# Folding the first head pair's decay terms into the 88-row contraction of its q k product

## The chip, the cores and the metric

The kernel runs on one core of one Trainium2 chip. A core has five engines that run side by side, each with its own instruction stream: TensorE (PE in the profile) for matrix products, VectorE (DVE), ScalarE (ACT), GpSimd (POOL) and SyncE (SP). POOL, SP and ACT also issue DMA transfers, which move data between the chip's memory and the on-chip buffers. The metric is the time of one execution on the device in microseconds (us), lower is better; a version's time is the median of its runs.

## The reference, cut to what matters

```python
scores = scale * np.matmul(q, k.transpose(0, 1, 3, 2))      # q, k, v: 8 batches, 8 heads, 576 tokens, 64 wide
log_f = np.log(np.clip(f, 0.0001, 1.0))                     # f: 8 x 8 x 576, a forget gate for each head and token
cum = np.cumsum(log_f, axis=-1)
decay = cum[:, :, :, None] - cum[:, :, None, :]
scores = np.where(causal, -1000000000.0, scores + decay)
attn = softmax(scores)                                      # (written out in the reference, with + 1e-09)
x = (attn @ v), heads side by side                          # 4608 tokens x 512
h = x @ w_in                                                # w_in: 512 x 2048
out = (h - np.tanh(h)) @ w_out                              # w_out: 2048 x 512, out: 4608 x 512 float32
```

What matters here is `decay`: to the score of query i and key j, cum at i is added and cum at j is taken away, for each head of each batch.

## The kernel before, in words

**Pairs and tiles.** The 64 heads (8 batches of 8) are worked in 32 pairs of heads. For a pair, q and k are transposed so that the 64 numbers of a head stand on 64 partitions (`trans`, L254 to L282: TensorE transposes at L264, then copies by VectorE or ScalarE at L275 and L277 into the tiles QT and KT). Scores are made key block by key block, transposed (keys on partitions), in seven tiles of a pair (TILES, L289), each of up to 512 columns in one PSUM bank (`scores`, L306): one product k q for each part of a tile (L326), in batch 0 a second small one that adds a mask to the diagonal blocks (L329, `late`), then exp by ScalarE (L335). `values` (L350) multiplies with v, VectorE normalises (L364 to L366), `turn` (L369) transposes the result into XR, and the MLP (`mlp1` L398 to L417, `mlp2_plain` and `mlp2` from L436) follows, spread between later pairs.

**The decay, from the second pair on.** QT and KT have three rows more than the 64 of the head: rows 64 to 66. KT has cum there in two fp16 parts (chi, the rounded value, and clo, the rest) and a row of ones; QT has two rows of -1 and a row cq with cum less a shift. One product over 67 rows so gives scale, decay and all. The constant rows come by SP's queue (L175 to L179), the others by `load_aug` (L168), for batch 0 on POOL's queue: from partition (batch, head) to row 64, 65 or 66 of every head.

**The decay, in the first pair.** These rows come too late for the first pair (`own`, L319). There the product runs over the 64 rows alone, and two matmuls for each part put the decay into PSUM first (`decay_part`, L294 to L298): one with the tile `dec` (chi and clo on 128 partitions) against a column `sel` that picks the head and changes the sign, one with a column of the identity against cq. The first tile's two are issued ahead (`decay(0)`, L529).

**The front.** f is loaded to 64 partitions (batch, head) by SP (L123), clipped by VectorE (L150), Ln by ScalarE (L157), summed up by a scan on VectorE (L159), rounded to chi (L162) and clo (L166); cq is made by ScalarE (L524). ScalarE needs a table load ahead of Ln and another ahead of exp (L525). `unread(n)` (L512) issues n matmuls of 128 columns whose result nobody reads, into which waits of TensorE fall.

**What sets the order.** Each engine works its instructions in the order in which the program emits them: `start()` (L521) emits the front and the first two tiles of pair 0, `bulk()` (L181) the rest of batch 0's loads, and then `att_items(p)` (L547) gives pair p's items: its seven tiles, the transposes of the next pair (`at_q` and `at_k` say behind which tile), loads (LOADS, L196) and the values of the pair before. POOL's queue in this order: q and k of heads 0 and 1 (L124, L125), of heads 2 and 3 (L132, L133), v of the last block and of heads 0 and 1 (L144 to L146), then `bulk`: q of heads 4 to 7, the three rows of `load_aug(0)` (chi L171, cq L172, clo L173), k of heads 4 to 7, four blocks of v; then batch 1's q and k, and w_in's first half (L189, placed at pair 1's tile 2). The first MLP matmul (L408) stands in pair 4's items behind tile 1.

Lines that say what words can't:

```python
    def load_aug(b):
        i, hs = b % 2, slice(b * H, (b + 1) * H)
        eng = nc.gpsimd if b == 0 else nc.sync
        eng.dma_start(out=KT[i][D:D + 1, :, 0:S], in_=chi[hs, :])
        eng.dma_start(out=QT[i][D + 2:D + 3, :, :], in_=cq[hs, :])
        eng.dma_start(out=KT[i][D + 1:D + 2, :, 0:S], in_=clo[hs, :])
```

Of the kernel before, what the change touches and what calls it, by code (L numbers as in the profile page):

```python
# [21 lines left out]
def kernel(  # L22
# [95 lines left out]
    def load_v_block(b, n, h0, h1):  # L118
# [3 lines left out]
    lf = TQ[0][0:NH, :, :].rearrange("p c s -> p (c s)").bitcast(FP32)[:, 0:S]  # L122
    nc.sync.dma_start(out=lf, in_=f.rearrange("b h s -> (b h) s"))  # L123
# [10 lines left out]
    ones16 = TK[0:NH, 0, :]  # L134
    sel = cst.tile([P, 2], FP16)
    dec = cst.tile([P, PITCH], FP16)
# [5 lines left out]
    nc.vector.memset(dec[:, S:PITCH], 0.0)  # L142
# [6 lines left out]

    nc.vector.tensor_scalar(out=lf, in0=lf, scalar1=0.0001, scalar2=1.0,  # L150
                            op0=ALU.max, op1=ALU.min)

    nc.vector.scalar_tensor_tensor(out=sel, in0=id16[:, 0:2], scalar=-1.0, in1=id16[:, NH:NH + 2],
                                   op0=ALU.mult, op1=ALU.subtract)
    nc.vector.memset(vn[0][D:P, NJ - 1, :, :], 0.0)
    nc.vector.memset(vn[0][:, :, :, D:VW], 1.0)
    nc.scalar.activation(out=lf, in_=lf, func=AF.Ln)  # L157
    cum = TQ[0][0:NH, :, :].rearrange("p c s -> p (c s)").bitcast(FP32)[:, S:2 * S]
    nc.vector.tensor_tensor_scan(out=cum, data0=ones16, data1=lf, initial=0.0,  # L159
                                 op0=ALU.mult, op1=ALU.add)  # L160
    chi = dec[0:NH, 0:S]
    nc.vector.tensor_scalar_mul(out=chi, in0=cum, scalar1=inv_qscale)  # L162
    cq = cst.tile([NH, S], FP16)
    expo = cst.tile([1, 1], FP32)
    clo = dec[NH:2 * NH, 0:S]
    nc.vector.scalar_tensor_tensor(out=clo, in0=cum, scalar=inv_qscale, in1=chi,  # L166
                                   op0=ALU.mult, op1=ALU.subtract)
    def load_aug(b):  # L168
        i, hs = b % 2, slice(b * H, (b + 1) * H)
        eng = nc.gpsimd if b == 0 else nc.sync  # L170
        eng.dma_start(out=KT[i][D:D + 1, :, 0:S], in_=chi[hs, :])  # L171
        eng.dma_start(out=QT[i][D + 2:D + 3, :, :], in_=cq[hs, :])  # L172
        eng.dma_start(out=KT[i][D + 1:D + 2, :, 0:S], in_=clo[hs, :])  # L173
# [120 lines left out]
    def decay_part(ps, a, j, i0, n, col):  # L294
        nc.tensor.matmul(out=ps[:, col:col + n], lhsT=dec[:, j * P:(j + 1) * P],
                         rhs=sel[:, a:a + 1].to_broadcast([P, n]), start=True, stop=False)
        nc.tensor.matmul(out=ps[:, col:col + n], lhsT=id16[0:NH, a:a + 1].to_broadcast([NH, P]),  # L297
                         rhs=cq[:, i0:i0 + n], start=False, stop=False)  # L298

    FIRST = []  # L300

    def decay(ti):
        FIRST.append(ps_sc.tile([P, 512], FP32, tag="sc", name="ps"))
        decay_part(FIRST[0], *TILES[ti][0])

    def scores(b, c, ti):  # L306
        if FIRST:
            ps = FIRST.pop()
        elif b == 0 and ti == LAST:
            ps = ps_tr.tile([P, UW], FP32, tag="tr", name="ps")  # L310
        else:
            ps = ps_sc.tile([P, 512], FP32, tag="sc", name="ps")
# [6 lines left out]
        own = b == 0 and c == 0  # L319
        rows = D if own else D + 3  # L320
        for a, j, i0, n, col in TILES[ti]:
            h = 2 * c + a
            if own and ti > 0:
                decay_part(ps, a, j, i0, n, col)
            cut = min(P, n) if b == 0 and i0 == j * P else 0
            nc.tensor.matmul(out=ps[:, col:col + n], lhsT=KT[b % 2][0:rows, h, j * P:(j + 1) * P],  # L326
                             rhs=QT[b % 2][0:rows, h, i0:i0 + n], start=not own, stop=cut == 0)
# [67 lines left out]
    def widen(n):  # L395
        turn_of[:] = [n, 0]
# [124 lines left out]
    def start():  # L521
        unread(33)
        q_rest = trans(*pairs[0], qn, QT, True, "AAAA", True)
        nc.scalar.activation(out=cq, in_=cum, func=AF.Copy, bias=-SHIFT * inv_qscale, scale=inv_qscale)  # L524
        nc.scalar.activation(out=expo, in_=lf[0:1, 0:1], func=AF.Exp)  # L525
        unread(6)
        k_rest = trans(*pairs[0], kn, KT, True, "VVVV", True)
        unread(22)
        decay(0)  # L529
        unread(8)  # L530
        scores(*pairs[0], 0)
        for fn in k_rest:
            fn()
        q_rest[0]()
        scores(*pairs[0], 1)
        q_rest[1]()
        for e in EL[0:2]:
            nc.vector.memset(e, 0.0)
        nc.vector.memset(KT[0][:, :, S:PITCH], 0.0)
# [7 lines left out]
    def att_items(p):  # L547
# [8 lines left out]
        for ti in range(len(TILES)):  # L556
# [5 lines left out]
            if early and p > 0 and ti in (0, 6):  # L562
                put(unread, 2)
# [4 lines left out]
            at_q, at_k = (1, 3) if p == 0 else (0, 1) if early else (0, 2) if p == NPAIR else (0, 3)  # L568
# [34 lines left out]
    FIVE = {PE, mybir.EngineType.Pool, mybir.EngineType.SP, mybir.EngineType.DVE, mybir.EngineType.Activation}  # L603
    with tc.manual_schedule(engines=FIVE):
        start()
    with tc.manual_schedule(engines=FIVE):
        bulk()
        for p in range(len(pairs) + 1):
            b, c = divmod(p, NPAIR)
            items = att_items(p)  # L610
            take = TAKE[p] if p < len(TAKE) else 8 - (p - len(TAKE)) % 2
            if p == 2 * NPAIR + 1:
                widen(1)
            mine = mlp[at:at + take]
            at += take
            first = 14 if p == NPAIR else 0
# [44 lines left out]
```

## Time and profile before

| | |
|---|---|
| median of 3 runs | 348.01 us (348.01 to 348.04) |
| the profiled execution | 347.95 us, of it 346.2 from the first to the last instruction (the span) |
| TensorE clock granted | 1.00 in every window |
| chain that ended last, by engine | PE 87%, DVE 6%, ACT 4% |
| same, by line, the largest | L408 32%, L466 28%, L326 12%, L357 8% |
| DMA | 38.80 MB, mean 112 GB/s |

The profile is that of one execution. For each engine it gives the busy time; the timeline gives instructions in order of time, each with its start, its length, its engine and line, the tile written and read, how many like it were merged, and in brackets how long the engine was idle ahead of it and what released it. The chain of waits is followed back from the last instruction and tells which work the end hung on. "PEld" is TensorE's load of the stationary operand, which may run beside a matmul. A line such as L408 is a line of the kernel as printed above.

### The profile page before, as it was taken

What the parts mean: (1) busy time and instruction counts of PE and PEld (TensorE: products, weight loads), DVE (VectorE), ACT (ScalarE), POOL (GpSimd) and SP (SyncE); (2) the same over time, 40 slices, a digit from 0 to 9 for tenths busy, and PEclk for the clock granted to TensorE, in tenths of its full rate; (3) what the DMA queues carried; (4) which work ended last, traced back from release to release, by engine and by line L of the source; (5) the groups of instructions that cost most, each with busy time, mean ns of one, the idle gap of its engine ahead of it and who ended that gap; (6) DMA issues with size and microseconds to landing.
All of it is one profiled execution on the core that took longest, in us unless ns stands there. A gap on an engine that the chain in (4) does not pass through costs nothing.

```text
span 346.2 us, 8606 instructions
## 1 busy us (share of the span) xinstructions
PE 335.2 (97%) x3253; PEld 230.6 (67%) x3253; DVE 261.7 (76%) x504; ACT 232.6 (67%) x437; POOL 161.3 (47%) x319
## 2 busy tenths in 40 slices
PE   8988998889999999999999999999999999999995
PEld 7476554555578656865688888755875587487485
DVE  6599787564988788678867886788677766876874
ACT  5687886777897787778767876788548842632640
POOL 8974652676558655765577465742322210000000
PEclk9999999999999999999999999999999999999999
DMA  8999999999999999799979997991131013003003
GB/s 108 147 182 201 193 201 154 107 114 177 132 130 105 177 137 122 94 176 137 117 78 200 130 128 78 186 143 27 49 97 31 17 50 110 0 14 109 0 11 113
DMA packets 144877, 38.80 MB, mean 112 GB/s; under 512 B 128148, under 2 KB 143236, under 8 KB 144836
## 3 DMA queue, kind: packets, MB, share of 16 engines
q0 software_dynamic: 92480, 18.39, 69.7%
q1 hardware_dynamic: 52356, 19.88, 30.5%
q8 instruction: 25, 0.41, 0.5%
q14 instruction: 16, 0.13, 0.1%
HBM read 36.85 MB, written 9.44 MB: 134 GB/s over the span
## 4 chain that ended last, share of the span: by engine, by line
PE 87%; DVE 6%; ACT 4%; issue 1%; DMA 1%; ACTq 0%
PE hps L408 32%; PE ops L466 28%; PE ps L326 12%; PE av L357 8%; PE ops L442 3%; DVE gq L417 2%; ACT e L335 2%; DVE QT L277 2%; PE t L264 1%; DVE KT L277 1%; PE ps L329 1%; DMA TQ<-in_f_dram 1%; PE ps L297 1%; ACT QT L275 1%; ACT th L413 1%
## 5 line engine op out<-in xcount | busy, mean ns | idle before, releaser
L408 PE MATMUL hps<-XR,win 128*128 128x512 f16 (+1 forms) x640 | 140.9, 357 | 0.9 <-ACT XR L378 0.7
L413 ACT ACTIVATE th<-hps 128x512 f32<-128x512 f32 x144 | 86.9, 603 | 55.4 <-PE hps L408 54.6
L335 ACT ACTIVATE e<-ps 128x512 f16<-128x512 f32 x192 | 110.5, 598 | 14.1 <-PE ps L326 6.0
L417 DVE TENSOR_TENSOR gq<-hps,th 128x512 f16<-128x512 f32 x144 | 98.4, 688 | 26.0 <-ACT th L413 24.6
L345 POOL TENSOR_SCALAR_AFFINE_SELECT e<-e 128x128 f16<-128x128 f16 x168 | 60.4, 361 | 78.0 <-ACT e L335 76.1
L408 PEld LDWEIGHTS <-win 128*128 128x128 f16 x640 | 57.7, 97 | 48.4 <-issue 0.5
L326 PE MATMUL ps<-QT,KT 67*128 67x64 f16 (+5 forms) x384 | 77.9, 276 | 3.1 <-ACT e L335 1.7
L466 PEld LDWEIGHTS <-gq 128*128 128x128 f16 x640 | 60.4, 97 | 11.1
L466 PE MATMUL ops<-wout,gq 128*128 128x256 f16 x512 | 63.2, 272 | 0.0
L326 PEld LDWEIGHTS <-KT 67*128 67x128 f16 (+1 forms) x384 | 36.7, 98 | 25.5 <-DVE KT L277 1.6
L357 PEld LDWEIGHTS <-e 128*128 128x128 f16 x896 | 32.2, 97 | 3.9
L357 PE MATMUL av<-vn,e 128*128 128x65 f16 x896 | 33.6, 193 | 0.0
L119 POOL DMA_DIRECT2D vn<-in_v_dram x32 | 28.0, 878 | 8.7 <-DMA win<-in_moe_w_in_dram 4.1
L466 PE MATMUL ops<-W,sq 128*128 128x256 f16 x256 | 31.2, 272 | 0.0
L366 DVE TENSOR_TENSOR xn<-av,rs 128x640 f16<-128x640 f32 x32 | 26.4, 825 | 1.1
L466 PEld LDWEIGHTS <-sq 128*128 128x128 f16 x256 | 24.2, 98 | 3.4
L96 POOL DMA_DIRECT2D kn<-in_k_dram x25 | 21.2, 848 | 1.5 <-issue 1.3
L345 POOL TENSOR_SCALAR_AFFINE_SELECT el<-el 128x128 f16<-128x128 f16 x28 | 9.4, 334 | 26.9 <-ACT el L335 26.2
L96 POOL DMA_DIRECT2D qn<-in_q_dram x25 | 21.2, 848 | 1.3 <-issue 0.8
L364 DVE TENSOR_SCALAR rs<-av 128x10 f32<-128x10 f32 x32 | 5.2, 162 | 19.0 <-PE av L357 17.9
L277 DVE COPY QT<-t 64x576 f16<-64x576 f16 x18 | 14.5, 803 | 6.2 <-PE t L264 6.1
L277 DVE COPY KT<-t 64x576 f16<-64x576 f16 (+1 forms) x22 | 16.3, 739 | 3.8 <-PE t L264 3.6
(82 smaller groups left out, 307.5 us busy)
## 6 DMA issues: line engine op xcount, KB each, us to landing
out_dram<-ost SPq DMA_DIRECT2D x34, 256.0 KB
vn<-in_v_dram POOLq DMA_DIRECT2D x24, 128.0 KB, 5.6
qn<-in_q_dram POOLq DMA_DIRECT2D x20, 128.0 KB, 4.3
kn<-in_k_dram POOLq DMA_DIRECT2D x20, 128.0 KB, 4.6
win<-in_moe_w_in_dram POOLq DMA_DIRECT2D x2, 1024.0 KB, 14.8
wout<-in_moe_w_out_dram POOLq DMA_DIRECT2D x2, 1024.0 KB, 14.1
XR<-xn SPq DMA_TRANSPOSE x56
vn<-in_v_dram POOLq DMA_DIRECT2D x12, 64.0 KB, 5.2
```

What stands on the lines that cost most here:

```text
L96: nc.gpsimd.dma_start(out=dst[b % 2][0:pn, n, :].rearrange("p (h d) -> p h d", h=H), in_=src[b, :, n * P:n * P + pn, :].rearrange("h p d - ...
L119: nc.gpsimd.dma_start(out=vn[b % 2][:, n, h0:h1, 0:D], in_=v[b, h0:h1, n * P:(n + 1) * P, :].rearrange("h p d -> p h d"))
L277: nc.vector.tensor_copy(out=to, in_=of)
L326: nc.tensor.matmul(out=ps[:, col:col + n], lhsT=KT[b % 2][0:rows, h, j * P:(j + 1) * P], rhs=QT[b % 2][0:rows, h, i0:i0 + n], start=not ow ...
L335: nc.scalar.activation(out=e[:, lo:hi], in_=ps[:, lo:hi], func=AF.Exp, scale=qscale)
L345: nc.gpsimd.affine_select(out=view, in_=view, compare_op=ALU.is_ge, fill=0.0, base=0, pattern=pat, channel_multiplier=-1)
L357: nc.tensor.matmul(out=av[:, a, ib, :], lhsT=E.pop((b, c, a, j, ib)), rhs=vn[b % 2][:, j, 2 * c + a, 0:D + 1], start=(j == 0), stop=(j == ib))
L366: nc.vector.tensor_tensor(out=xn.rearrange("p i (a d) -> p a i d", a=2), in0=av[:, :, :, 0:D], in1=rs.to_broadcast([P, 2, NJ, D]), op=ALU. ...
L408: nc.tensor.matmul(out=hps[:, o:o + n], lhsT=win[:, ci, ft * P:(ft + 1) * P], rhs=XR[:, ci, t:t + n], start=(ci == 0), stop=(ci == NCH - 1))
L413: nc.scalar.activation(out=th, in_=hps, func=AF.Tanh, scale=-1.0)
L417: nc.vector.tensor_tensor(out=GQ[(u, i)][:, half, kt, :], in0=hps, in1=th, op=ALU.add)
L466: nc.tensor.matmul(out=ps[:, m, :], lhsT=LHS[lhs](u, kt // 4)[:, kt % 4, m * P:(m + 1) * P], rhs=rhs[:, kt, :], start=(fresh and (apart or ...
```

## The change: one contraction over 88 rows

For the first pair, the 64 rows of the head and 24 rows of decay terms stand in one tile, so that one product over 88 rows gives the whole score, and the two decay matmuls of each part go. The 24 rows are made where they are needed: f's eight rows of batch 0 are loaded a second time, three times over, to partitions 64 to 87, by ScalarE's queue; clip, Ln and scan run over 88 partitions instead of 64. Three groups of eight rows follow: on K's side -chi, ones, clo (by per-partition factors mul_k, add_k, mul_l), the same for both heads; on Q's side for head h a one in row h of the first group, cum less the shift in row h of the second, a -1 in row h of the third, and zeros elsewhere (by mul_0, add_0, mul_1, add_1). The factors are made from the identity tile by eleven small VectorE operations. The first pair's operands are KS and QS, which lie in the space of the weights W1 and W2 that are filled later. Also: `load_aug` issues clo ahead of cq; clo is made by VectorE after the first two copies of k; the exp table load stands right behind Ln; K's padding memset stands at the front; the transposes of k for pair 2 stand behind pair 1's tile 3 instead of tile 1; and the idle matmuls are 91 instead of 69 up to pair 1.

```diff
+    NX = NH + 3 * H
+    lf = TQ[0][0:NX, :, :].rearrange("p c s -> p (c s)").bitcast(FP32)[:, 0:S]
+    nc.sync.dma_start(out=lf[0:NH, :], in_=f.rearrange("b h s -> (b h) s"))
+    nc.scalar.dma_start(out=lf[NH:NX, :], in_=bass.AP(f.tensor, f.offset, [[0, 3], [S, H], [1, S]]))
...
+    nc.vector.memset(KT[0][:, :, S:PITCH], 0.0)
+    chi = cst.tile([NX, S], FP16)
+    clo = cst.tile([NH, S], FP16)
+    cq = cst.tile([NH, S], FP16)
+    KS = W1.rearrange("p k e -> p (k e)")[:, 0:2 * PITCH].rearrange("p (a n) -> p a n", a=2)
+    QS = W2.rearrange("p k e -> p (k e)")[:, 0:2 * S].rearrange("p (a n) -> p a n", a=2)
+    nc.vector.memset(KS[0:NX, :, S:PITCH], 0.0)
+    per = cst.tile([NX, 9], FP32)
+    isb, isc, mul_k, add_k, mul_l, mul_0, add_0, mul_1, add_1 = (per[:, i:i + 1] for i in range(9))
...
+    for to, i in ((isb, H), (isc, 2 * H)):
+        nc.vector.tensor_reduce(out=to, in_=id16[0:NX, NH + i:NH + i + H], op=ALU.add, axis=mybir.AxisListType.X)
+    nc.vector.tensor_scalar(out=mul_k, in0=isb, scalar1=-inv_qscale, scalar2=inv_qscale, op0=ALU.mult, op1=ALU.add)
+    nc.vector.tensor_scalar_mul(out=add_k, in0=isb, scalar1=-1.0)
+    nc.vector.tensor_scalar_mul(out=mul_l, in0=isc, scalar1=inv_qscale)
     nc.vector.tensor_scalar(out=lf, in0=lf, scalar1=0.0001, scalar2=1.0, op0=ALU.max, op1=ALU.min)
-    nc.vector.scalar_tensor_tensor(out=sel, in0=id16[:, 0:2], scalar=-1.0, in1=id16[:, NH:NH + 2], ...)
     nc.vector.memset(vn[0][:, :, :, D:VW], 1.0)
+    for h, (mul, add) in enumerate(((mul_0, add_0), (mul_1, add_1))):
+        nc.vector.tensor_scalar_mul(out=mul, in0=column(H + h), scalar1=inv_qscale)
+        nc.vector.scalar_tensor_tensor(out=add, in0=mul, scalar=-SHIFT, in1=column(h), op0=ALU.mult, op1=ALU.add)
+        nc.vector.tensor_tensor(out=add, in0=add, in1=column(2 * H + h), op=ALU.subtract)
     nc.scalar.activation(out=lf, in_=lf, func=AF.Ln)
+    nc.scalar.activation(out=expo, in_=lf[0:1, 0:1], func=AF.Exp)
     nc.vector.tensor_tensor_scan(out=cum, data0=ones16, data1=lf, ...)
-    nc.vector.tensor_scalar_mul(out=chi, in0=cum, scalar1=inv_qscale)
-    nc.vector.scalar_tensor_tensor(out=clo, in0=cum, scalar=inv_qscale, in1=chi, op0=ALU.mult, op1=ALU.subtract)
+    nc.vector.tensor_scalar(out=chi, in0=cum, scalar1=mul_k, scalar2=add_k, op0=ALU.mult, op1=ALU.add)
+    nc.vector.scalar_tensor_tensor(out=KS[NH:NX, 0, 0:S], in0=cum[NH:NX, :], scalar=mul_l[NH:NX, :], in1=chi[NH:NX, :],
+                                   op0=ALU.mult, op1=ALU.subtract)
     def load_aug(b):
         eng.dma_start(out=KT[i][D:D + 1, :, 0:S], in_=chi[hs, :])
+        eng.dma_start(out=KT[i][D + 1:D + 2, :, 0:S], in_=clo[hs, :])
         eng.dma_start(out=QT[i][D + 2:D + 3, :, :], in_=cq[hs, :])
-        eng.dma_start(out=KT[i][D + 1:D + 2, :, 0:S], in_=clo[hs, :])
...
     def scores(b, c, ti):
+        kt, qt, rows = (KS, QS, NX) if b == 0 and c == 0 else (KT[b % 2], QT[b % 2], D + 3)
         for a, j, i0, n, col in TILES[ti]:
-            if own and ti > 0:
-                decay_part(ps, a, j, i0, n, col)
+            nc.tensor.matmul(out=ps[:, col:col + n], lhsT=kt[0:rows, h, j * P:(j + 1) * P],
+                             rhs=qt[0:rows, h, i0:i0 + n], start=True, stop=cut == 0)
...
     def start():
+        def row_q(h, mul, add):
+            nc.scalar.activation(out=QS[NH:NX, h, :], in_=cum[NH:NX, :], func=AF.Identity, bias=add[NH:NX, :], scale=mul[NH:NX, :])
         unread(33)
-        q_rest = trans(*pairs[0], qn, QT, True, "AAAA", True)
-        nc.scalar.activation(out=cq, in_=cum, func=AF.Copy, ...)
-        nc.scalar.activation(out=expo, in_=lf[0:1, 0:1], func=AF.Exp)
+        row_q(0, mul_0, add_0)
+        q_rest = trans(*pairs[0], qn, (QS,), True, "AAAA", True)
+        row_q(1, mul_1, add_1)
+        nc.scalar.activation(out=cq, in_=cum[0:NH, :], func=AF.Copy, ...)
         unread(6)
-        k_rest = trans(*pairs[0], kn, KT, True, "VVVV", True)
-        unread(22)
-        decay(0)
-        unread(8)
+        k_rest = trans(*pairs[0], kn, (KS,), True, "VVVV", True)
+        unread(32)
         scores(*pairs[0], 0)
+        unread(4)
+        nc.vector.scalar_tensor_tensor(out=clo, in0=cum[0:NH, :], scalar=inv_qscale, in1=chi[0:NH, :], ...)
+        nc.vector.tensor_copy(out=KS[NH:NX, 1, 0:S], in_=KS[NH:NX, 0, 0:S])
         for fn in k_rest:
             fn()
         q_rest[0]()
         scores(*pairs[0], 1)
+        unread(4)
         q_rest[1]()
...
-            if early and p > 0 and ti in (0, 6):
-                put(unread, 2)
+            if early and ti in (0, 6) or p == 0 and ti == 5:
+                put(unread, 2 if p else 4)
-            at_q, at_k = (1, 3) if p == 0 else (0, 1) if early else ...
+            at_q, at_k = (1, 3) if p == 0 else (0, 3) if p == 1 else (0, 1) if early else ...
```

The whole program now stands under one hand-ordered schedule instead of two after the front (`manual_schedule`).

## The prediction

> **What bounds the kernel now.** I read the page first, then the chain of waits, then the timeline of the first 60 us by engine. Part 1 of the page says TensorE is nearly always busy:
>
> ```profile
> PE 335.2 (97%) x3253; PEld 230.6 (67%) x3253; DVE 261.7 (76%) x504; ACT 232.6 (67%) x437; POOL 161.3 (47%) x319
> ```
>
> That is an average. The change touches the first pair alone, so only the first 17 us and what they start matter. The timeline there (start, us, engine, line; in brackets the idle time before and its releaser):
>
> ```profile
> 0.81 1.28 ACT L157 ACT_TABLE_LOAD   x1 [0.81 <-PEq L645]
> ...
> 3.55 0.54 DVE L150 TENSOR_SCALAR TQ<-TQ 64x576 f32<-64x576 f32 x1 [0.71 <-DMA TQ<-in_f_dram]
> ...
> 4.11 0.68 ACT L157 ACTIVATE TQ<-TQ 64x576 f32<-64x576 f32 x1 [2.02 <-DVE TQ L150]
> ...
> 4.83 1.35 DVE L159 TENSOR_TENSOR_SCAN TQ<-TK,TQ 64x576 f32<-64x576 f16 x1 [0.66 <-ACT TQ L157]
> ...
> 6.96 0.75 DVE L166 SCALAR_TENSOR_TENSOR dec<-TQ,dec 64x576 f16<-64x576 f32 x1
> ...
> 7.82 1.96 DVE L277 COPY KT<-t 64x288 f16<-64x288 f16 x4
> ...
> 9.96 0.70 POOL L90 DMA_DIRECT2D kn<-in_k_dram  x1
> ...
> 13.32 0.39 PE L297 MATMUL ps<-cq,id 64*128 64x512 f16 x1
> ```
>
> Read down: up to 7.9 us a chain of f, clip, Ln, scan and two roundings runs. From then to 16.23, where pair 1 starts, TensorE itself is the chain, two decay matmuls like that of L297 ahead of each product. From there VectorE sets the pace: its copies of successive pairs start at 17.07, 21.56 and 26.05, that is 4.49 us per pair with 99% busy. The last fact is the one that I take to decide. POOL's timeline, its idle time, and the load's time to landing (last column):
>
> ```profile
> 16.67 0.83 POOL L189 DMA_DIRECT2D win<-in_moe_w_in_dram  x1
> ...
> 30.79 0.82 POOL L119 DMA_DIRECT2D vn<-in_v_dram  x1 [4.11 <-DMA win<-in_moe_w_in_dram]
> ```
> ```profile
> win<-in_moe_w_in_dram POOLq DMA_DIRECT2D x1, 1024.0 KB, 13.8
> ```
> ```profile
> 31.98 0.81 PE L408 MATMUL hps<-XR,win 128*128 128x512 f16 x3
> ```
>
> The first half of w_in lands at 16.67 + 13.8 = 30.47 and the first MLP matmul, which needs it, starts at 31.98 without idle time: 1.5 us of room, no more. Behind that matmul the chain goes through TensorE, ACT and VectorE to 56.6 us, then TensorE to the end, so the total moves with the start of that matmul.
>
> **TensorE's work in pair 0.** 24 decay matmuls go. In the chain from 0 to 18 us L295 has 9.1% and L297 14.4%: 1.64 + 2.59 = 4.2 us. 22 more idle matmuls come (91 for 69), at 1.39/22 = 0.063 us each 1.4 us; ten of them stand ahead of the first score in a wait that is there anyway (below), twelve between scores. The 88-row product takes no longer than the 64-row one: the 512-column form with 67 rows takes 0.38, the one with 64 rows 0.39. So TensorE alone would save some 3 us in pair 0. If nothing else bound, that would be the gain.
>
> **The front gets later.** In the instruction order of the changed kernel the Ln table load now waits for both landings of f; before it ran at 0.81, free. f landed at 3.52 (0.81 + 2.71 in the chain). The 24 repeated rows go out on ACT's queue; I let them land with the others, since SP's 64 rows issue at the same 0.81. Then the load takes 3.55 to 4.83 and Ln starts at 4.85 instead of 4.11. Eleven small VectorE operations on 88x1 are new. The nearest rows are 128x10: 0.17 and 0.22, 0.21 to 0.25 from start to start when one needs the other; the bottom is the 0.09 of a small memset. Five stand ahead of the clip, hidden by the table load; six stand between clip and scan, where Ln (to 5.53) hides most. The scan then starts between 5.56 and 6.1; I take 5.75. From there: scan 1.38, chi 0.73, the 24-row subtraction 0.75 (as the 64-row form), two head-0 copies of k 0.98, clo 0.75. The sum puts the end of **clo at 10.35** (bounds 10.15 to 10.7; it was 7.71) and the first score near 9.65 instead of 9.14. ACT does the second table load (1.28), two new 24x576 rows (0.66 as cq), two copies and cq by about 10; so its first exp slips from 9.72 to about 10.1.
>
> The Trainium skill ("ScalarE: Activation LUTs", What ACT_TABLE_LOAD costs) gives 1.28 us for a load and 1.38 us more for a drain at each switch. By that sentence Ln, and with it clo, would come 1.4 us later still; here the load at 7.47 is followed by an activation at 8.77, so this trace shows the 1.28 alone.
>
> **Pair 0 and pair 1.** VectorE follows clo with the copy of the 24 rows to head 1 (not in the trace: between 0.11 for a memset and 0.75 for an operation of that length; 0.4), the head-1 copies 0.98, memsets 0.24, and the copies for pair 1, 1.61 + 1.60. That ends at 15.2, where pair 1 may start: 1.0 us before 16.23. The memset of K's padding moved ahead of f, where VectorE waits (0.71 idle), and costs nothing. Pair 1 also needs cq's rows by POOL's DMA: issue near 10.9, landing 3.4 (fastest v load) to 5.1 (cq now) later, 14.3 to 16.0. So pair 1 gains 0.2 to 1.05, and I take 1.0 because few loads are then under way. That is all that the 3 us leave, since VectorE's pace rules the next three pairs. TensorE would reach the first MLP matmul at 31.0.
>
> **POOL's queue.** Its order was chi, cq, clo, kn. Now clo stands second. POOL stands in it until clo is done, then issues clo and cq (0.55 each, so 1.1) and then the second half of k: 10.35 + 0.05 + 1.1 = 11.5 instead of 9.96. Behind it wait four v loads, batch 1's q and k and w_in, issued back to back, so they all slip by **1.5 us**: w_in goes out at 18.2. Does its landing slip as much? The windows of one microsecond (the column ahead of the last is the DMA share):
>
> ```profile
> 10.00:11.00 1.00, 1.00 (x13) 0.55 (x11) 0.26 (x1) 0.94 (x3) 1.00 (x2) 1.00 1.23 194
> 11.00:12.00 1.00, 1.00 (x9) 0.33 (x6) 0.88 (x2) 0.83 (x2) 1.00 (x2) 1.00 0.69 82
> 12.00:13.00 1.00, 1.00 (x17) 0.74 (x16) 0.71 (x1) 0.65 (x2) 1.00 (x2) 1.00 0.88 127
> 13.00:14.00 1.00, 1.00 (x9) 0.28 (x6) 0.79 (x1) 0.23 (x1) 1.00 (x3) 1.00 1.57 175
> ```
>
> From 12.4 to 30 the DMA engines are full, so engines that stand idle in the pause of 11 to 12.4 lose the whole 1.5. But the share in the pause is not zero, and clo's 9 KB, issued at 9.46, take 4.7 us to land: some engine was behind until 14.2, and it uses the longer pause to catch up. A load has landed when its slowest part has. So the slip lies between 0 and 1.5; I take **1.0**, two thirds, because only a part of the engines works in the pause. w_in lands at 31.5, the first MLP matmul starts near 31.55 instead of 31.98.
>
> The Trainium skill ("DMA: Bandwidth & Descriptors", Queues, rings and completion order) says that a DMA is split over up to 16 engines with a ring each. By it the slowest engine sets the landing, which speaks for a slip under 1.5; no row here shows one engine alone.
>
> **Sum.** TensorE ready at 31.0, w_in at 31.55: the later one counts, 31.98 - 31.55 = 0.4 us gained. Behind it nothing moves twice: the fourth v block of batch 1, whose issue waits for w_in, lands at 30.8 + 8.8 = 39.6 now and would land near 40.6, against its use from 41.3 (40.9 then); this is a second reason why more than 1 us is hard to gain. SP's queue has the same transfers with clo and cq exchanged; its wait there is for batch 1's rows, not needed before 29.8. The profiled execution took 347.95 (span 346.2 and 1.75 around it), 0.06 under the median of 348.01. So 347.95 - 0.4 + 0.06: **347.6 us**.
>
> **Rivals.**
> - *w_in slips whole* (1.5): lands at 31.97 and the start is 32.0: 348.0. For it: full DMA engines from 12.4. Chance 0.22.
> - *w_in hardly slips*: the late engine is the last in both kernels. Then the gain is what VectorE's chain leaves, 0.7 to 1.3: 346.7 to 347.3, middle 347.0. For it: clo's 4.7 us. Chance 0.25.
> - *Slower*: POOL is held longer in front of clo. Every microsecond later costs a microsecond once w_in lands after 31.9, that is for clo after 10.3 if the slip is whole, 10.8 if it is two thirds. Its price: with f's repeated rows landing 1 us late, clo at 11.35, w_in at 32.5 to 33.0, +0.5 to +1.0: 348.5 to 349.0. For it: ACT's queue is not in the trace. Against it: f's load took 2.71 with the queues empty. The table load with a drain is the same case: clo at 11.7, +0.8 to +1.4, up to 349.4. Together 0.13, of which the drain has 0.02.
> - *TensorE's saving counts whole*: 348.0 - 3.0 = 345.0. Against it: VectorE's 99% from 17 us and w_in. Chance 0.02.
>
> The forecast (347.3 to 347.9) has 0.38. A measurement of this kernel tells some 0.2% (0.7 us) from no change. Faster by more: the second and the last rival and the forecast's edge, 0.31. Slower by more: 0.09. Within: 0.60. The range reaches from the no-slip case to the lower part of the slower one, 346.8 to 348.5.
>
> **What would show it.** Right: a table load on ACT at 3.5, Ln at 4.85; clo's end near 10.3; POOL's k load near 11.5 and w_in's at 18.2; an idle time of TensorE before the first L408-type MLP matmul, put to DMA win, or none and a start near 31.5; pair 1's first score near 15.2. Wrong: w_in out before 17.5, TensorE not waiting there and the start before 31; or idle TensorE in pair 1 for its decay rows.

## The result and the profile after

| kernel | median, us | runs | ratio to before, same chip |
|---|---|---|---|
| before | 348.04 (348.00 to 349.70) | 22 | 1 |
| after | 349.15 (348.36 to 352.24) | 22 | 1.0035 [1.0023, 1.0047] |

The change made the kernel slower by 0.35%, 1.1 us. The forecast was 347.6 with a range of 346.8 to 348.5; the result lies above the range, on the side that had a chance of 0.09. The spread is new too: nearly all runs of before lie within 0.1 us, those of after over 3.9 us. The execution that was profiled took 352.24 us (span 350.5, clock 0.990) and is the longest of them, so the total of its parts is larger than the 1.1 us to be explained. A run more than 1.5% above the fastest of its kernel belongs to a slower state and is left out of medians and ratios below: 891 us in e4, 353.0 and 353.9 in e7, 354.9 in e15.

Part 1 of the page of after:

```profile
PE 334.3 (95%) x3251; PEld 231.2 (66%) x3251; DVE 263.7 (75%) x516; ACT 234.8 (67%) x439; POOL 162.4 (46%) x319
```

TensorE works 0.9 us less than before, though a part of it at half the clock (below), and the kernel is longer: the lost time shows as waiting. The timeline of the front, all engines (start, us, engine, line; in brackets the idle time before and its releaser), against the lines shown of before:

```profile
0.81 1.38 ACTq L127 DMA_DIRECT2D TQ<-in_f_dram  x1
...
4.31 0.46 DVE L169 TENSOR_SCALAR TQ<-TQ 88x576 f32<-88x576 f32 x1 [0.62 <-DMA TQ<-in_f_dram]
4.35 1.28 ACT L176 ACT_TABLE_LOAD   x1 [4.35 <-DMA TQ<-in_f_dram]
...
5.65 0.69 ACT L176 ACTIVATE TQ<-TQ 88x576 f32<-88x576 f32 x1
...
6.37 1.35 DVE L180 TENSOR_TENSOR_SCAN TQ<-TK,TQ 88x576 f32<-88x576 f16 x1 [0.68 <-ACT TQ L176]
6.60 1.21 POOL L158 TENSOR_SCALAR_AFFINE_SELECT late<-late 128x128 f16<-128x128 f16 x1
...
7.86 0.86 ACT L524 ACTIVATE W<-TQ,per 24x576 f16<-24x576 f32 x1
...
10.20 0.75 DVE L536 SCALAR_TENSOR_TENSOR clo<-TQ,chi 64x576 f16<-64x576 f32 x1
...
10.22 0.39 PE L327 MATMUL ps<-W,W 88*128 88x512 f16 x1 [1.82 <-DVE W L295]
...
12.25 0.70 POOL L90 DMA_DIRECT2D kn<-in_k_dram  x1
```

The landing of f's 24 repeated rows holds VectorE and ScalarE until 4.31; f was there at 3.52 before. Clip, table load, Ln and scan follow one behind the other, clo ends at 10.95 (7.71 before), TensorE idles 1.82 us ahead of its first score, and POOL, which goes on 0.29 behind clo's end, issues the k load at 12.25 (9.96 before). The chain of waits up to 35 us tells where that goes (start, us, what):

```profile
8.63 0.53 POOL KT L189
9.16 2.07 issue
11.22 0.02 POOLq L191
11.24 0.52 POOL KT L190
11.76 0.50 POOL QT L191
12.26 0.69 POOL kn L90
12.95 3.32 POOL vn L119 x4
16.27 0.65 POOL qn L90
16.91 0.64 POOL kn L90
17.56 0.74 POOL qn L90
18.30 0.66 POOL kn L90
18.96 14.51 DMA win<-in_moe_w_in_dram
```

Read from the end: the first MLP matmul waits for w_in, w_in waits in POOL's queue behind nine loads of k, v and q, and these wait behind the 2.07 us in which POOL stands ahead of clo. In before this chain ran through TensorE. On TensorE's own timeline that matmul shows the wait:

```profile
33.52 0.82 PE L409 MATMUL hps<-XR,win 128*128 128x512 f16 x3 [1.81 <-DMA win<-in_moe_w_in_dram]
```

It starts 1.54 later than before (31.98), and TensorE was ready at 33.52 - 1.81 = 31.7. The windows behind it (busy time and count of PE, PEld, DVE, ACT, POOL; granted clock; DMA share; GB/s), after:

```profile
30.00:35.00 5.00, 3.07 (x50) 2.20 (x49) 3.06 (x7) 2.06 (x5) 1.24 (x3) 0.97 1.48 198
35.00:40.00 5.00, 4.37 (x18) 2.06 (x17) 2.54 (x4) 3.08 (x7) 2.78 (x6) 0.50 1.68 184
40.00:50.00 10.00, 10.00 (x86) 5.42 (x85) 7.45 (x13) 6.54 (x14) 7.03 (x12) 0.92 1.29 206
```

The granted clock falls to 0.50 behind the wait; before had 1.00 there. At 60.8 us after stands 4.2 us behind before (60.79 against 56.57, the same score): 1.54 from the start of the MLP, the other 2.7 behind it, where the clock was low.

### The profile page after: what moved, and what is told of

It reads as the page before. It is cut to its first block, busy times and chain, and to the rows that moved or that the text cites. A ratio compares the mean times of both kernels' runs of the same rounds, so it can differ in the third digit from the quotient of the medians.

```text
span 350.5 us, 8619 instructions
## 1 busy us (share of the span) xinstructions
PE 334.3 (95%) x3251; PEld 231.2 (66%) x3251; DVE 263.7 (75%) x516; ACT 234.8 (67%) x439; POOL 162.4 (46%) x319
## 4 chain that ended last, share of the span: by engine, by line
PE 84%; POOL 4%; DMA 4%; DVE 3%; ACT 2%; issue 2%; POOLq 0%; ACTq 0%
PE hps L409 35%; PE ops L467 28%; PE ps L327 10%; PE av L358 7%; DMA win<-in_moe_w_in_dram 4%; PE ops L443 3%; DVE QT L295 1%; POOL vn L119 1%; PE t L282 1%; POOL qn L90 1%; POOL kn L90 1%; DVE gq L418 1%; ACT QT L293 1%; DVE KT L295 1%; ACT e L336 1%
## 5 line engine op out<-in xcount | busy, mean ns | idle before, releaser
L409 PE MATMUL hps<-XR,win 128*128 128x512 f16 (+1 forms) x640 | 143.1, 361 | 2.5 <-DMA win<-in_moe_w_in_dram 1.8
L327 PE MATMUL ps<-QT,KT 67*128 67x512 f16 (+1 forms) x372 | 75.4, 279 | 3.4 <-ACT e L336 1.7
L327 PEld LDWEIGHTS <-KT 67*128 67x128 f16 x372 | 35.8, 99 | 26.3 <-issue 2.4
L295 DVE COPY KT<-t 64x576 f16<-64x576 f16 x18 | 14.3, 797 | 5.1 <-PE t L282 4.9
L295 DVE COPY QT<-t 64x576 f16<-64x576 f16 x18 | 14.4, 803 | 4.0 <-PE t L282 3.9
## 6 DMA issues: line engine op xcount, KB each, us to landing
wout<-in_moe_w_out_dram POOLq DMA_DIRECT2D x2, 1024.0 KB, 15.2
```

Source lines behind the costliest of these rows:

```text
L295: nc.vector.tensor_copy(out=to, in_=of)
L327: nc.tensor.matmul(out=ps[:, col:col + n], lhsT=kt[0:rows, h, j * P:(j + 1) * P], rhs=qt[0:rows, h, i0:i0 + n], start=True, stop=cut == 0)
L409: nc.tensor.matmul(out=hps[:, o:o + n], lhsT=win[:, ci, ft * P:(ft + 1) * P], rhs=XR[:, ci, t:t + n], start=(ci == 0), stop=(ci == NCH - 1))
```

## The experiments

Two causes were to be told apart, and their source found. Theory A: POOL waits ahead of clo, and so w_in lands late. Theory C: TensorE's waits let the granted clock fall. Rivals: the fold's chain itself is longer, or its gain is lost in other waits of the first pair. Each kernel was timed in five rounds; a ratio is to before on the same chip. It goes by the mean of the runs, not by their median, so a few long runs raise it. A statement on the clock or on a wait is one on the profiled execution, unless it names the runs.

### 1. Batch 0's decay rows issued by SP (e1)

```diff
-        eng = nc.gpsimd if b == 0 else nc.sync
+        eng = nc.sync
```

> The changed kernel, with batch 0's three decay rows (chi, clo, cq) issued by SP's queue, so that POOL goes from the second half of q straight to the second half of k. Theory A (POOL stands in front of clo, so k, v and w_in go out 2.3 us late, w_in lands after TensorE needs it and TensorE waits): k out near 8.6 instead of 12.25, w_in out near 15.3 instead of 18.96, landed by 30.5 or earlier, no wait of TensorE ahead of the first MLP matmul, its start at 31.0 to 31.5, total 347.0 to 347.8. Theory B (the fold itself costs: the later front, ACT's and VectorE's extra work): the total stays near 349.1, with w_in in time. Theory C (a cold TensorE clock from idle time in pair 0): stays near 349, with a clock under 1 before 20 us.

Measured: 348.35 (347.79 to 352.45), ratio 1.0024 [0.9997, 1.0051]. In its profile (347.87 us, clock 1.00) w_in goes out at 15.97, and the first MLP matmul starts at 32.12 with no wait for it. The 1.8 us wait is gone, as theory A has it. But the time misses the 347.0 to 347.8 that it expected, and 32.12 is no better than before's 31.98: pair 1's first score stands at 16.39, after 0.80 us of waiting for cq's row. Ahead of the first score TensorE waits 2.11 us here, and the clock stays at 1.00. And two of 12 runs took 352.2 and 352.5, at a clock of 0.99, though the wait for w_in was gone.

### 2. f's repeated rows by SP, too (e2)

```diff
-    nc.scalar.dma_start(out=lf[NH:NX, :], in_=bass.AP(f.tensor, f.offset, [[0, 3], [S, H], [1, S]]))
+    nc.sync.dma_start(out=lf[NH:NX, :], in_=bass.AP(f.tensor, f.offset, [[0, 3], [S, H], [1, S]]))
```

> The changed kernel, with the second load of f (24 rows) issued by SP behind the first one instead of by ACT. Theory A: the rows land at 3.9 to 4.4 instead of 4.29; if at 3.9, table load, Ln, scan, clo and with them k and w_in come 0.4 us earlier, total 348.7; if SP's second issue lands no earlier, nothing changes (349.1). Theory B: the same size of step, since the front comes earlier by as much. It tells how much of the delay is ACT's queue and how much a second DMA of f by any queue.

Measured: 350.83 (350.34 to 351.31), ratio 1.0083 [1.0070, 1.0096]. As the second load on SP's queue the rows come at 5.78, 1.47 later than by ScalarE's and far outside the 3.9 to 4.4 expected. On VectorE's timeline:

```profile
5.78 0.46 DVE L169 TENSOR_SCALAR TQ<-TQ 88x576 f32<-88x576 f32 x1 [2.06 <-DMA TQ<-in_f_dram]
```

w_in goes out at 20.36, lands near 34.2, and the first MLP matmul starts at 34.26. TensorE itself comes to it only 0.16 earlier: it waited 3.01 us ahead of its first score, and the clock is 0.50 from 12 to 15 us behind that. The rows' landing is a lever on the whole front, and ScalarE's queue was the better of the two.

### 3. The wait put into the kernel before (e3)

```diff
         load_aug(0)
+        for _ in range(4):
+            nc.gpsimd.memset(KT[1][:, :, S:PITCH], 0.0)
         load_qk(kn, k, 0, 4, H)
```

> The kernel before, with four memsets of 0.6 us (padding that is set later anyway) on POOL between the three decay rows and the second half of k: nothing but POOL's queue is held, by 2.3 us. Theory A: w_in goes out near 19.0 and lands near 33, TensorE waits 1 us or more ahead of the first MLP matmul, total 348.9 to 349.8 although no other part of the change is in it. Theories B and C: 348.0, since neither front nor fold is there.

Measured: 348.29 (347.94 to 349.53), ratio 1.0015 [1.0006, 1.0025]. The memsets held POOL for 1.5 us net (k load at 11.48, w_in at 18.17). The profiled execution (349.19, clock 1.00) starts its first MLP matmul at 33.19 after 1.06 us of waiting for w_in: the late w_in costs its time with no fold at all. But the median misses the 348.9 to 349.8 expected: the runs fall into two groups, eight of 347.9 to 348.5 and four of 349.2 to 349.5. So holding POOL does not always cost that much. Only one execution was profiled, one of the longer ones; what the others do differently stays open.

### 4. The wait for w_in filled (e4)

28 idle matmuls ahead of the first MLP matmul of after (`put(unread, 28)`).

> The changed kernel, with 28 idle matmuls ahead of the first MLP matmul, which fill the wait for w_in and change nothing else. The profile of the changed kernel shows granted clock 0.50 from 35 to 40 us, behind a wait of 1.8 us. If the long times of the changed kernel (up to 352) come from the clock that falls in that wait: the clock stays 1.00, the highest time comes down to 349.5 and the median to 348.9. If the clock falls for another reason, the spread stays. Theory A expects the wait for w_in itself to remain (start near 33.5), so the median does not come back to 348.0.

Measured: 349.32, four runs within 349.24 to 349.35, ratio 1.0039 [1.0026, 1.0052]. The window behind the wait, two lines of TensorE's timeline and one of POOL's:

```profile
35.00:40.00 5.00, 4.32 (x28) 2.17 (x27) 3.46 (x6) 4.18 (x10) 2.15 (x6) 1.00 1.69 183
```
```profile
31.79 1.74 PE L516 MATMUL idle<-warm 128*128 128x128 f16 x28
33.36 0.81 PE L409 MATMUL hps<-XR,win 128*128 128x512 f16 x3
```
```profile
32.77 0.82 POOL L119 DMA_DIRECT2D vn<-in_v_dram  x1 [4.11 <-DMA win<-in_moe_w_in_dram]
```

The clock stays at 1.00 and the runs lie close together; runs above 350, as the profiled one of after with its low clock, did not occur in these few. The time is not won back, but e4 does not tell what the late w_in costs. Here w_in, issued at 18.96 as in after, took 13.5 us and had landed by 32.5 (POOL, which waits for it, goes on at 32.77). TensorE still worked on the 28 idle matmuls then, and these hold the first MLP matmul until 33.36. The runs of after itself tell more: 13 of the 22 had a clock of 1.00 and took 348.36 to 349.57, median 349.08. So after loses 1.0 us without a fall of the granted clock; its three runs above 350 all had a lower one.

### 5. Before without its decay matmuls (e5), and with idle ones in their place (e11)

```diff
-                decay_part(ps, a, j, i0, n, col)
...
+            if p == 0 and ti > 1:
+                put(unread, 8)
```

e5 has the first line (the first tile's two go as well); e11 has both, with eight idle matmuls after each of the first two tiles as well.

> The kernel before without its 24 decay matmuls (the first pair's scores lack their decay), nothing put in their place: the most that their removal from TensorE can be worth. Theory A1 (pair 0 is bound by TensorE, as the chain of before says): pair 1 starts at 15.0 or earlier, limited by its decay rows that land at 14.2 and by VectorE's copies, and the first MLP matmul moves from 31.98 to 30.6 to 31.0: total 346.6 to 347.0. Theory D (pair 1 is held by loads or by VectorE anyway): pair 1 starts at 16.0 or later, total 347.8 to 348.0.

> The kernel before without its 24 decay matmuls (as e5; the first pair's scores lack their decay) and with 8 idle matmuls (8 x 0.06 = 0.5 us) after each of the first pair's tiles, 56 in all, so that TensorE is kept busy without the fold's additions. Theory C: with the idle matmuls the clock stays 1.00, pair 1's first score stands between e5's 13.82 and before's 16.23, and the first MLP matmul then waits for w_in (landed 30.5 in before and in e5), so the median is 346.6 to 347.5: this is the most that the removed TensorE work can be worth, with the MLP's weights as the next bound. Rival (the removed matmuls are worth nothing, the first pair is bound by VectorE, ScalarE and the DMAs): first MLP at 31.9 or later with a warm clock and 347.9 to 348.2. If the clock falls all the same, clocks of 0.98 to 0.99 and about 348.1 as in e5.

Measured: e5 348.13 (347.95 to 350.47), ratio 1.0017 [1.0002, 1.0032], with a clock of 0.98 to 0.99 in every run. Pair 1 starts at 13.82, 2.4 us earlier than before, and then:

```profile
14.00:17.00 3.00, 3.00 (x29) 2.43 (x28) 1.71 (x3) 1.81 (x4) 3.00 (x6) 0.50 2.02 157
17.00:24.00 7.00, 6.85 (x70) 5.49 (x68) 4.45 (x8) 3.99 (x8) 6.48 (x11) 0.50 1.15 165
```

Ten microseconds at half the clock eat the 2.4 us up; the first MLP matmul starts at 33.56. The removed matmuls had kept the clock up. No wait of TensorE is listed from 5 to 14 us, so this fall does not stand behind a wait. e11 took 348.91 (348.88 to 349.12), ratio 1.0027 [1.0016, 1.0038], clock 1.00: that the idle matmuls hold the clock is confirmed. The busy share does not tell the two apart: from 8 to 14 us TensorE is busy for 5.67 us in e5 and for 5.27 in e11. What does stays open. But they were too many. TensorE was busy through the first pair and the first MLP matmul started at 33.02 without a wait, so e11 tells nothing on the worth of the removed work.

### 6. The second load of f left out (e8)

```diff
-    nc.scalar.dma_start(out=lf[NH:NX, :], in_=bass.AP(f.tensor, f.offset, [[0, 3], [S, H], [1, S]]))
...
+    nc.vector.memset(lf[NH:NX, :], 0.9)
```

> The changed kernel without the second load of f: the 24 rows are set to a constant by VectorE (the first pair's decay is then wrong), all else as in the changed kernel. Theory A with its source in the second load (f's 24 rows land at 4.29 instead of 3.52, and the table load waits for them): clip at 3.9, Ln at 4.8 instead of 5.65, clo's end at 10.1 instead of 10.95, w_in out at 18.1 instead of 18.96, first MLP matmul at 32.4 to 32.7, total 348.3 to 348.7. If the second load costs nothing beyond its landing and other work holds the front: under 0.3 from the changed kernel's 349.15.

Measured: 348.74 (347.85 to 351.50), ratio 1.0032 [1.0014, 1.0050]; after's is 1.0035 [1.0023, 1.0047], so the times alone do not tell the two apart, and what follows rests on the profile. In f's landing this is the kernel that the prediction reckoned with. Three lines of its timelines (TensorE, POOL, TensorE):

```profile
15.09 0.39 PE L327 MATMUL ps<-QT,KT 67*128 67x512 f16 x1 [0.34 <-DVE KT L295]
```
```profile
18.25 0.83 POOL L207 DMA_DIRECT2D win<-in_moe_w_in_dram  x1
```
```profile
32.71 0.82 PE L409 MATMUL hps<-XR,win 128*128 128x512 f16 x3 [1.70 <-DMA win<-in_moe_w_in_dram]
```

Pair 1 at 15.09 (predicted 15.2), w_in out at 18.25 (18.2), TensorE ready at 32.71 - 1.70 = 31.0 (31.0). The landing differs: 32.7, not 31.5. The clock stays at 1.00 behind this wait of 1.70.

### 7. Mending w_in, cq and the first wait (e6, e7, e9, e10, e12)

e6 issues w_in's first 256 columns ahead of batch 1's q load; e7 is e1 with cq made and issued first; e9, e10 and e12 are e1, e7 and e6 with 30 idle matmuls more ahead of the first score:

```diff
-             (0, 4): [lambda: load_qk(qn, q, 1, 2, H)],
+             (0, 4): [lambda: load_win(0, 256), lambda: load_qk(qn, q, 1, 2, H)],
...
-             (1, 2): [lambda: load_win(0, DFF // 2)],
+             (1, 2): [lambda: load_win(256, DFF // 2)],
...
-        unread(32)
+        unread(62)
```

> The changed kernel, with the first 256 of w_in's columns (256 KB) loaded ahead of the big load of batch 1's q instead of with the others: the first two MLP matmuls no longer wait for the whole first half. Theory A (the wait for w_in is what the change loses): no wait ahead of the first MLP matmul, its start at 31.7, where TensorE is ready in the changed kernel, clock 1.00, total 347.6 to 347.8, that is 1.4 less than the changed kernel. If the next loads (k of batch 1, w_in's rest) are late by the moved 256 KB, 348.0 to 348.5. Theory B (the fold's own cost): 349.

> Like the run with batch 0's rows on SP's queue, but cq is made by ACT ahead of the second Q row and goes out ahead of clo. There pair 1 started at 16.39, behind 0.80 of waiting for cq's landing. If that wait is all that holds pair 1: cq goes out near 10.7, clo at 11.3, pair 1 starts at 15.9 (VectorE's copies end there), first MLP matmul at 31.6, total 347.5 to 347.6. If clo's landing takes over (4.5 us from its issue at 11.3): 15.8 to 16.0, the same within 0.1. If VectorE's and ACT's chain hold it at 16.3: 347.9.

> The kernel after with the first batch's decay rows issued by SP (as in e1) and 62 instead of 32 idle matmuls ahead of the first score (30 x 0.065 = 1.9 us, the length of TensorE's wait there in e1, 2.11). Theory C (the granted clock falls in some executions because TensorE waits 1.8 to 2.1 us ahead of the first score): the wait shrinks to under 0.4, the clock is 1.00 in the profile and in all runs, the runs near 352 of e1 are gone, and the median is what e1's start of the first MLP (32.12) gives with a warm clock, 347.9 to 348.1: the same as before. Rival, that the slow executions of e1 come from the thin work of the whole first pair (the 0.77 and 0.80 us waits after the first score) and not from this one wait: the spread stays, clocks of 0.98 to 0.99 in some runs, median 348.3.

> As e9, with cq made before the second head's row and its DMA ahead of clo's (as in e7, whose undisturbed runs took 347.35 and whose others 348.3 to 353.9). Theory C: all runs at clock 1.00 and a median of 347.3 to 347.6, 0.1 to 0.2% faster than before; this is the fold without its late w_in and without the fall of the clock. Rival (the clock falls in the thin first pair whatever stands in front of the first score): two groups of times again, median above 348.2.

> The kernel after with the first columns of w_in issued ahead (as e6, profiled with the first MLP matmul at 31.60 and no wait) and 62 instead of 32 idle matmuls ahead of the first score. Theory A with C: both of the fold's costs are gone while its rows stay on POOL, clock 1.00 in all runs, first MLP at 31.6 to 31.8, and so 347.95 - 0.3 = 347.5 to 347.8, a little faster than before. Rival (more idle matmuls only hold up the first score, or w_in's second part is late for the second MLP group): 348.0 or more, with the clock at 1.00.

| kernel | median (range), us | ratio | first MLP matmul |
|---|---|---|---|
| e6 | 348.34 (347.67 to 349.14) | 1.0012 [1.0003, 1.0020] | 31.60, no wait |
| e7 | 349.42 (347.35 to 351.17) | 1.0039 [1.0014, 1.0065] | 32.02, no wait |
| e9 | 348.17 (347.83 to 350.89) | 1.0019 [1.0002, 1.0036] | 32.12, no wait |
| e10 | 347.68 (347.57 to 350.98) | 1.0005 [0.9989, 1.0021] | 33.07, no wait |
| e12 | 347.89 (347.38 to 351.50) | 1.0005 [0.9988, 1.0023] | 31.43, no wait |

e6 shows theory A with the rows still on POOL: no wait, and 0.8 us better than after (its profile, of a run of 348.77, has a later wait of 1.55 us for a k load, which now stands behind the first part of w_in). e10's profile is of one of its longer executions (348.86): its 62 idle matmuls took 5.24 us instead of e9's 3.63 and held the first score up to 12.12, so its 33.07 is not that of the median. From 7 to 10 us it issued 12 to 14 matmuls in a microsecond where e9 issued 21 to 22, and both profiles give the granted clock as 1.00 there: a listed 1.00 does not rule out half pace. In e7 the two runs at a clock of 1.00 took 347.35 and 347.41, the eight others, at 0.985 to 0.995, 347.86 to 351.17. In its profile the clock falls within a microsecond behind the 2.16 us wait ahead of the first score: 0.58 from 10 to 14 us. Filling that wait (e10 against e7) brings the median down by 1.7 us, with 10 of 11 runs at a clock of 0.999 or more, which is what theory C says. It does not end the spread: one run in 11 or 12 stays above 350 in e10 and e12, two of 12 in e9. The one of e12, 351.50, has a clock of 1.00, so the granted clock is not behind all of the long runs. e9 shows again that SP's rows cost the fold's gain, now by cq's wait of 0.88 us.

### 8. All three costs taken away at once, a control, and a longer first fill (e13 to e16)

e13 is e12 with e8's edit; e14 is before with e6's edit; e15 and e16 are e10 and e12 with 45 for 33 idle matmuls at the start.

> The kernel after without the second load of f (its 24 rows are filled with 0.9, so the first pair's decay is not the real one; every later operation is there), with the first columns of w_in issued ahead as in e12 and 62 idle matmuls ahead of the first score. If the fold's chain is worth what the prediction said once f's rows, w_in and the clock don't hold it: pair 1's first score at 15.0 to 15.2 (e8: 15.09), first MLP matmul at 30.9 to 31.0 without a wait, 347.0 us (347.95 - 1.0), clock 1.00. Rival (pair 1 is held by VectorE's copies and ScalarE's exps, and f's rows cost nothing more by then): 31.4 to 31.6 as in e12, 347.4 to 347.6.

> The kernel before with the first 256 columns of w_in issued ahead of the second batch's q load, as in e6 and e12. If w_in is not what bounds the kernel before (it landed at 30.47 and TensorE came to it at 31.98): the same time, 347.9 to 348.0, ratio 0.9995 to 1.0005. Rival, that the early w_in is itself worth the 0.3 us by which e12's warm runs lie under before: 347.5 to 347.7.

> e10 with 45 instead of 33 idle matmuls at the very start, so that TensorE does not pause 0.6 us ahead of the first transposes of q (e10's profile shows half pace from 5.5 to 12 behind that pause, and its first score 1.8 us late). If the spread of e9 and e10 comes from that pause: all runs within 347.5 to 347.75 and a ratio of 0.999 with an interval under 1. Rival (the clock follows the work of the first microseconds as a whole, or f's landing sets the spread): runs above 348.4 as before, interval over 1.

> e12 with the same 45 idle matmuls at the start. If that pause makes the spread: runs within 347.35 to 347.6, ratio 0.9985 to 0.999. Rival: 347.4 to 348.6 as in e12, with the clock at 1.00, because the landing of f's 24 rows moves from run to run and all of the first pair hangs on it.

Measured: e13 347.20 (346.95 to 347.90), ratio 0.9981 [0.9972, 0.9990]; e14 347.93 (347.91 to 347.96), ratio 0.9999 [0.9990, 1.0008]. TensorE in e13, with no wait for w_in:

```profile
30.85 0.94 PE L409 MATMUL hps<-XR,win 128*128 128x512 f16 x3
```

With f's rows, w_in and the clock out of the way the first MLP matmul starts 1.1 us earlier than before and the time falls by 0.8. e14 shows that an early w_in alone moves nothing (first MLP matmul at 31.98, as before): the gain comes from the changed first pair, fold and reordering together. e15 took 348.62 (347.96 to 349.11), ratio 1.0019 [1.0010, 1.0028], e16 348.86 (348.43 to 349.58), ratio 1.0026 [1.0015, 1.0038]. The longer fill did not end the spread, and both medians are 0.9 to 1.0 higher, so the pause ahead of the first transposes alone is not its cause. In e16's profile f's rows come at 4.70 instead of e12's 4.20, the first MLP matmul starts at 32.00 instead of 31.43, and the last output addition waits 1.38 us for a store; why they do so was not found.

No version that computes the first pair's whole decay was shown to be faster than before: e10 and e12 have 0.1 to 0.3 us less in the median, with intervals on both sides of 1.

## Why the prediction was wrong, step by step

**What bounds the kernel: right.** Where nothing is lost later, the time goes with the start of the first MLP matmul, 347.95 + (start - 31.98): e13's 30.85 gives 346.8 (measured 346.95), e12's 31.43 gives 347.4 (347.39), e3's 33.19 gives 349.2 (349.19), e4's 33.36 gives 349.3 (349.31), e2's 34.26 gives 350.2 (350.34). After's profile lies above it by 2.7 (the clock), e6's by 1.2 (the later k load) and e16's by 0.9 (the store).

**TensorE's work: right in what was measured.** The 88-row product takes 0.39, as the 64-row one; the 3 us as a whole were not measured by themselves. What the step left out is that this work kept the clock up (e5).

**The front: the first failed step.** "I let them land with the others": the rows came at 4.31, not 3.52, and Ln at 5.65, not 4.85. The scan so starts at 6.37, not 5.75, and clo ends at 10.95, not 10.35; from the scan's start to clo's end it is 4.58, as summed (4.59), and TensorE's first score came at 10.22, not 9.65. ScalarE's two 24-row products took 0.86 each, not 0.66, and its first exp came at 11.33, not 10.1; that lies beside the chain to clo. e8 gives the price: without the second load w_in goes out 0.7 earlier. The bounds given for clo (10.15 to 10.7) left the load out, though ScalarE's queue was named as unknown further down. The drain of a table load of which the Trainium skill speaks ("ScalarE: Activation LUTs", What ACT_TABLE_LOAD costs) did not show: Ln starts 0.02 after its load ends.

**Pair 0 and pair 1: right on its condition.** TensorE was to be ready at 31.0 and was at 31.7, so the gain was 0.3 instead of 1.0. With f on time it was 31.0 (e8), and pair 1 began at 15.09 against 15.2 forecast. The mechanism, VectorE's copies behind clo, was the right one. cq's rows took 2.2 us to land, less than the bounds of 3.4 to 5.1, and did not hold pair 1.

**POOL's queue: the second failed step, and the larger.** The issue was forecast at 18.2 and came at 18.25 with f on time, in part by luck: in e8 clo ended 0.1 us before the sum, and POOL went on 0.29 behind it, not 0.05. But "I take 1.0, two thirds" for the landing was wrong. The forecast leaves w_in 13.3 us from issue to landing (31.5 - 18.2); before took 13.8, after 14.5, e8 14.4, e3 15.0, e2 13.9, e4 13.5. So the landing slipped by about as much as the issue or by more: 3.0 for 2.3 in after, 2.2 for 1.6 in e8, 2.7 for 1.5 in e3, 3.7 for 3.7 in e2, 2.0 for 2.3 in e4. In four of the five that is at or above the upper bound given, the whole of the issue's slip. These are single executions: the eight shorter runs of e3, at most 348.5, leave by the rule above a start of 32.5 at most, so a slip of 2.0 or less. The windows of one microsecond show why nothing was caught up in the pause; after:

```profile
10.00:11.00 1.00, 0.78 (x9) 0.57 (x10) 0.94 (x3) 0.99 (x2) 0.00 (x0) 1.00 0.99 149
11.00:12.00 1.00, 0.94 (x18) 0.82 (x17) 0.97 (x3) 0.98 (x3) 0.76 (x2) 1.00 0.78 129
12.00:13.00 1.00, 0.54 (x9) 0.41 (x6) 0.97 (x4) 0.98 (x3) 1.00 (x3) 1.00 0.13 28
13.00:14.00 1.00, 0.69 (x11) 0.57 (x11) 0.99 (x2) 0.97 (x3) 1.00 (x2) 1.00 0.40 34
```

From 12 to 14 us the engines move 28 and 34 GB/s where before moved 127 and 175: the engines as a whole stood nearly idle (DMA share 0.13 and 0.40), so little was caught up there; what a single engine did no row shows. From 10 to 14 that is 340 KB instead of 576. After had moved 395 KB less than before in the stretch from 10 to 30 us, 2.0 us at the 199 GB/s that before has at its end; for e8 it is 321 KB (1.6 us), for e3 379 KB (1.9 us), for e4 374 KB (1.9 us), for e2 836 KB (4.2 us). That is 0.7 to 1.1 of each slip, so the volume not moved accounts for most of it. Part of it arises from 17 to 24 us (153 GB/s in after, 174 in before), when the queue is full again; the reason for that stays open. With f on time, this step alone makes the 347.6 into 348.7 (e8's profile).

**The clock: not in the sum at all.** The prediction held the 1.00 of before for given. After's idle times of 1.8 us ahead of the first score and ahead of the MLP go with a fall in some executions: 1.81 us of waiting, then 0.50 from 35 to 40. e1's 2.11 and e8's 1.70 were not followed by one, and e5's fall has no listed wait ahead of it. The granted clock goes with the long runs of after; the 1.0 us lost at a clock of 1.00 it does not explain. The Trainium skill ("TensorE: Matmul & The Clock Gate", What's actually happening) has a half-rate state that follows at least one idle window of about 3.4 us. The 0.50 agrees, and so does the cure by idle matmuls in e4; the length does not, the waits here are half as long, in stretches where TensorE was busy for 60%, and e5 has none.

**The rivals.** The slower one, POOL held longer by late rows of f, is what happened: its case of rows 1 us late gave 348.5 to 349.0, and rows 0.8 us late gave 349.15. It had 0.13 because f's first load was taken as evidence for the second, and because the slip was taken for two thirds of the issue's.

## What to carry to other kernels

A load that is made a second time has a landing of its own; bound it by the slowest load of that size near it, not by the first one, when a chain begins with it. Before an issue queue is made to wait, look at what is queued behind the wait and count the whole slip for the last transfer (here 0.9 to 1.8 times the issue's), unless the DMA engines are seen to stay busy through the pause. And work that is taken off an engine which had no waits leaves waits or thinner work behind: the clock may fall there, so look at the granted clock, and fill the waits, before the saving is counted.

## What the runs showed of the hardware

- **Landing by queue.** 54 KB in 24 rows, issued at 0.81 us, came at 4.2 to 4.7 us by ScalarE's queue in the kernels that had it there, and at 5.78 as the second load on SP's.
- **Operands by partition.** ScalarE's 24x576 product with scale and bias as columns took 0.86 us; cq over 64x576 with constants took 0.69 in the same profile.
- **POOL beside VectorE's scan.** A 128x128 select on POOL that starts while the scan runs ends 0.08 to 0.09 us behind the scan's end, whenever it started: in after 6.60 to 7.81 (scan to 7.72), in e12 6.58 to 7.68 (7.60), in e8 6.61 to 7.09 (7.01). In e16 it starts at 6.59, 0.16 ahead of the scan, takes 0.36 and ends inside it, and the scan takes 1.42 instead of 1.35. In before, with the scan over, it took 0.45 instead of after's 1.21, by which after's next load of q goes out at 7.77 instead of 7.03. It seems that the two do not get on side by side and that the later one waits.
- **Rows of a product.** In before, a 512-column product over 64 rows is followed by one over 128 rows after 0.32 us (9.14 to 9.46); in after, the one over 88 rows after 0.23 (10.22 to 10.45). The weight loads stand out of cover in the first case. So the 88-row form is cheaper than its length of 0.39 tells.
- **Clock and waits.** Behind single waits of TensorE of 1.8 to 3.0 us the granted clock fell to 0.50 (after, e7, e2), and behind others of 1.7 and 2.1 us it did not (e8, e1). In e5 it fell with no listed wait.
